# Attention scores of two heads from 64 rows of TensorE each, three split terms, two chunks in a burst

## The chip, the core and the metric

The kernel runs on one core of a Trainium2 chip. The metric is the device time of one execution in microseconds (us); three executions of the kernel before took 1080.8, 1082.9 and 1083.42 us, and their median, 1082.9 us, is the time before.

## What is computed

Sigmoid attention over 8 batches of 12 heads (448 tokens, 64 elements per head), followed by a feed-forward part without a nonlinearity:

```
scores = scale * np.matmul(q, k.transpose(0, 1, 3, 2)) - np.log(S)
attn = 1.0 / (1.0 + np.exp(-scores))
attn_out = np.matmul(attn, v)
x = attn_out.transpose(0, 2, 1, 3).reshape(B * S, H * D)
a = x @ w1
b = x @ w2
h = a * b @ w3
out = h @ w_out
```

The attention works in float32; the weights are float64 words, which the kernel decodes itself.

## The kernel before, in words

Two heads that stand side by side are a *pair*; there are 6 pairs per batch and 48 in all. The 448 tokens of k are cut into four *chunks*, three of 128 and one of 64 (the short chunk, number 3). For a chunk, TensorE makes the scores of both heads: a PSUM tile `sp` of two banks, one per head, with k's tokens down the partitions and 448 q tokens along. Two `sp` tiles exist, so that a third one waits until the first has been read. ScalarE takes the sigmoid, and TensorE multiplies the result with v (`attend`, accumulated in `av`).

The first 9 pairs are *plain*: q, k and the attention are float32, and one matmul per head makes a chunk's scores, from the 64 partitions in which that head's elements lie (line 196). The other 39 pairs are *split*: a value is the sum of a high part, rounded to fp32r, and the rest, its low part. Of q, a tile `qs` holds one head per column block, with the high part in partitions 0 to 63 and the low part in 64 to 127; k lies twice in `kh` (high) and twice in `kl` (low), once for either half of the partitions. So a matmul over all 128 rows multiplies one part of k with both parts of q, and a full chunk needs four matmuls (two heads, `kh` and `kl`, line 199). For this q and k are loaded twice each, by four DMAs per pair (line 135). The short chunk packs `kh` and `kl` into one tile `ks` of 128 columns (GpSimd, line 165), needs two matmuls (line 225), and has its two halves added by ScalarE and VectorE (`add_halves`, lines 186 and 187) before its sigmoids (`short_attention`). `attention` takes the sigmoid of a full chunk twice, rounded into `ah` and exact back into `sp`, and VectorE writes the difference to `al` (line 217).

Each pair has four *slots*, one per chunk, in the order 0, 3, 1, 2. In a slot TensorE's program has the scores of that slot's chunk; then 12 matmuls of the *filler* `up` (line 318), which is the first feed-forward product of the batch before; then the `attend` of the chunk of the slot before (line 255; four matmuls for a full chunk of a split pair, two for the short one). The orders of TensorE and of SP, which issues the DMAs, are written out by hand like this. From slot 34 on, a scheduler orders ScalarE, VectorE and GpSimd. `prepare` says in which slot a pair is loaded and split. Slot 36 is the first of the split pairs.

After the last pair TensorE finishes `up` (line 318), multiplies w3 with w_out (line 508) and makes the output (line 524).

Of the kernel before, what the change touches and what calls it, by code (L numbers as in the profile page):

```python
# [11 lines left out]
F32 = mybir.dt.float32  # L12
F32R = mybir.dt.float32r
U32 = mybir.dt.uint32
AF = mybir.ActivationFunctionType
ALU = mybir.AluOpType
# [9 lines left out]
def sigmoid_attention_bilinear_ffn(  # L26
# [16 lines left out]
    nc = tc.nc  # L43
    B, H, D, S = qT.shape
    DM, DF = w1.shape[0], w1.shape[1] // 2
    NT = B * S
    P = 128
    CHUNKS = [(c, min(P, S - c)) for c in range(0, S, P)]
    NC = len(CHUNKS)
    assert 2 * D == P and CHUNKS[-1][1] == D  # L50
    NPAIR = H // 2
# [4 lines left out]
    PLAIN = 9  # L56
# [3 lines left out]
    ps = ctx.enter_context(tc.tile_pool(name="ps", bufs=3, space=PSUM))  # L60
# [4 lines left out]
    def split(dst_hi, dst_lo, src, hi_engine, lo_engine):  # L65
        hi_engine(out=dst_hi, in_=src)  # L66
        lo_engine.tensor_tensor(out=dst_lo, in0=src, in1=dst_hi, op=ALU.subtract)  # L67
# [43 lines left out]
    pa = phase_a.enter_context(tc.tile_pool(name="pa", bufs=2, side="right"))  # L111
# [10 lines left out]

    def load_pair(b, hp):
        heads = slice(2 * hp, 2 * hp + 2)
        if b * NPAIR + hp < PLAIN:

            qk = pa.tile([P, 2, S], F32, name="qp", tag="qk", bufs=3)
            for i, src in enumerate((qT, kT)):
                nc.sync.dma_start(out=qk[:, i], in_=src[b, heads].rearrange("h d s -> (h d) s"))
            return qk[:, 0], qk[:, 1]  # L130
        qq = pa.tile([P, 2, S], F32, name="qq", tag="qk", bufs=3)
        kk = pa.tile([P, 2, S], F32, name="kk", tag="qk", bufs=3)
        for dst, src in ((qq, qT), (kk, kT)):
            for r in range(2):
                nc.sync.dma_start(
                    out=dst[r * D:(r + 1) * D], in_=src[b, heads].rearrange("h d s -> d h s")
                )
        return qq, kk

    def load_v(b, hp):  # L140
        vv = pa.tile([P, NC, 2 * D], F32, name="vv")
# [6 lines left out]
            nc.sync.dma_start(out=vv[r * D:(r + 1) * D, NC - 1], in_=v[b, full:, cols])  # L148
        return vv

    def split_pair(plain, qq, kk):

        if plain:
            return qq, kk, None, None
        qs = pf[0].tile([P, 2, S], F32R, name="qs")
        kh = pf[0].tile([P, 2, S], F32R, name="kh")
        kl = pf[0].tile([P, 2, S], F32R, name="kl")
        nc.vector.tensor_copy(out=qs, in_=qq)
        nc.vector.tensor_tensor(out=qs[D:], in0=qq[D:], in1=qs[D:], op=ALU.subtract)
        split(kh, kl, kk, nc.vector.tensor_copy, nc.gpsimd)  # L160

        ks = pf[0].tile([P, 2, P], F32R, name="ks")
        for j in range(2):
            for i, k in ((j, kh), (1 - j, kl)):
                nc.gpsimd.tensor_copy(out=ks[:, j, i * D:(i + 1) * D], in_=k[:, j, S - D:])
        return qs, kh, kl, ks

    def split_v(plain, vv):
        if plain:
            return vv  # L170

        vs = pf[0].tile([P, NC, 2, 2, D], F32R, name="vs")
        for j in range(2):
            split(vs[:, :, j, j, :], vs[:, :, j, 1 - j, :], vv[:, :, j * D:(j + 1) * D],
                  nc.vector.tensor_copy, nc.gpsimd)
        return vs

    def sigmoid(dst, src):
        n = src.shape[0]
        nc.scalar.activation(dst, src, AF.Sigmoid, bias=bias[:n], scale=scale)  # L180

    def add_halves(dst, src):

        for j in range(2):
            rows, others = slice(j * D, (j + 1) * D), slice((1 - j) * D, (2 - j) * D)
            nc.scalar.copy(out=dst[rows], in_=src[j][others])  # L186
            nc.vector.tensor_tensor(out=dst[rows], in0=src[j][rows], in1=dst[rows], op=ALU.add)  # L187

    def scores(qs, kh, kl, c):

        at, n = CHUNKS[c]
        sp = ps.tile([P, 2, 512], F32, name="sp", bufs=2)[:n, :, :S]
        for j in range(2):
            if kl is None:
                rows = slice(j * D, (j + 1) * D)
                nc.tensor.matmul(sp[:, j], kh[rows, at:at + n], qs[rows], start=True, stop=True)  # L196
                continue
            for m, k in enumerate((kh, kl)):
                nc.tensor.matmul(sp[:, j], k[:, j, at:at + n], qs[:, j], start=m == 0, stop=m == 1)  # L199
        return sp  # L200

    def attention(plain, sp):

        n = sp.shape[0]
        if plain:
            a = pa.tile([P, 2, S], F32, name="ap", tag="ah", bufs=3)[:n]
            sigmoid(a, sp)
            return (a,)
        ah = pa.tile([P, 2, S], F32R, name="ah", tag="ah", bufs=3)
        sigmoid(ah[:n], sp)  # L210
        sigmoid(sp, sp)
        if n < P:

            nc.vector.tensor_tensor(out=ah[n:], in0=sp, in1=ah[:n], op=ALU.subtract)
            return (ah,)
        al = pf[0].tile([P, 2, S], F32R, name="al")
        nc.vector.tensor_tensor(out=al, in0=sp, in1=ah, op=ALU.subtract)  # L217
        return ah, al

    def short_scores(ks, qs):  # L220


        sp = ps.tile([P, 2, 512], F32, name="sp", bufs=2)[:, :, :S]
        for j in range(2):
            nc.tensor.matmul(sp[:, j], ks[:, j], qs[:, j], start=True, stop=True)  # L225
        t = pf[0].tile([P, S], F32, name="st", bufs=1)
        add_halves(t, [sp[:, j] for j in range(2)])
        return t

    def short_attention(t):  # L230

        a = pa.tile([P, 2, S], F32R, name="ah", tag="ah", bufs=3)
        for j in range(2):
            rows = slice(j * D, (j + 1) * D)
            sigmoid(a[rows, j], t[rows])
        sigmoid(t, t)
        for j in range(2):
            rows, others = slice(j * D, (j + 1) * D), slice((1 - j) * D, (2 - j) * D)
            nc.vector.tensor_tensor(out=a[others, j], in0=t[rows], in1=a[rows, j], op=ALU.subtract)  # L239
        return (a,)  # L240

    def attend(c, ops, v, accs):

# [89 lines left out]
    def take(stream, n):  # L333
        for _ in range(n):
            next(stream, None)
# [30 lines left out]
    qks, vvs = {}, {}  # L366
    for p in range(2):
        qks[p] = load_pair(*pairs[p])
        load_job(p)
        if p == 0:  # L370
            vvs[0] = load_v(*pairs[0])
    splits, vs = {0: split_pair(0 < PLAIN, *qks.pop(0))}, {0: split_v(0 < PLAIN, vvs.pop(0))}
    xs = {b: [] for b in range(B)}
    filler = iter(())
    waiting = []
    accs = {}
    pf = []
# [14 lines left out]
    def prepare(p, i):  # L392

        n = p + 1
        change = n in (PLAIN, PLAIN + 1)
        if i == (2 if change else 1) and n < len(pairs):
            splits[n] = split_pair(n < PLAIN, *qks.pop(n))
        if i == 0 and change:
            qks[n] = load_pair(*pairs[n])
        if i == 1 and n < len(pairs):  # L400
            vvs[n] = load_v(*pairs[n])
        if i == NC - 1 and n < len(pairs):
            vs[n] = split_v(n < PLAIN, vvs.pop(n))
        n = p + 2
        if i == (0 if n < PLAIN else 2) and n not in (PLAIN, PLAIN + 1) and n < len(pairs):
            qks[n] = load_pair(*pairs[n])
# [3 lines left out]
    chunks = [0, NC - 1, *range(1, NC - 1)]  # L410
    ups = -(-(NF * 2 * NK * 3) // (NPAIR * NC))
    slot = 0
    for p, (b, hp) in enumerate(pairs):
        plain = p < PLAIN
        qs, kh, kl, ks = splits.pop(p)
        for i, c in enumerate(chunks):
            if slot == PLAIN * NC - 2:
                order.close()
                order.enter_context(tc.manual_schedule(engines={ET.PE, ET.SP}))
                phase_p.close()  # L420
                pf.append(phase_a.enter_context(tc.tile_pool(name="pf", bufs=2, side="right")))
            prepare(p, i)
            if not plain and i == 1:
                short = short_scores(ks, qs)
            else:
                sp = scores(qs, kh, kl, c)
                if not plain and i == 2:
                    waiting.append((slot + 1, p, NC - 1, short_attention(short)))
                waiting.append((slot + 1, p, c, attention(plain, sp)))
            for step, n in steps.get(slot, ()):  # L430
                step(n)
            if b > 0 and (hp, i) == (0, 2):
                take(filler, 10 ** 6)
                filler = up(b - 1, xs[b - 1], itertools.repeat("up"))
            take(filler, ups)
            if slot == 1:
                idle_products(6)
            attend_due(slot)
            slot += 1
# [21 lines left out]
    for jc in range(NF):  # L461
        take(filler, 10)
        for half in range(2):
            ms = slice(half * NM, (half + 1) * NM)
            src = w_out[jc * P:(jc + 1) * P].rearrange("p (m u) -> p m u", u=2)[:, ms]
# [33 lines left out]
    for ic in range(NF):  # L499
# [3 lines left out]
        for half in range(2):  # L503
            ms = slice(half * NM, (half + 1) * NM)
            acc = ps.tile([P, 512], F32, name="up", tag=next(banks), bufs=2)
            for jc in range(NF):
                for m, (a, w) in enumerate(((w3h, woh), (w3h, wol), (w3l, woh))):
                    nc.tensor.matmul(  # L508
                        acc[:, :NM], a[:, jc], w[:, jc, ms],
                        start=(jc == 0 and m == 0), stop=(jc == NF - 1 and m == 2),  # L510
# [52 lines left out]
```

## Time and profile before

| | |
|---|---|
| Span of the profiled execution, first to last instruction | 1079.5 us |
| Times of the runs | 1080.8, 1082.9, 1083.42 us |
| TensorE busy with matmuls | 1067.9 us |
| VectorE, ScalarE, GpSimd busy | 714.1, 563.4, 190.1 us |
| DMA packets' time, share of 16 engines' span | 40.6% |
| Mean granted clock of TensorE | 0.998 |

The span leaves out what lies ahead of the first and behind the last instruction, so a time is a little longer than a span. In the rows of the profile PE is TensorE's matmul, PEld its weight load, DVE VectorE, ACT ScalarE, POOL GpSimd, and L199 is line 199 of the kernel. "128\*128" is the part of the array that an instruction uses, rows by columns. The plain pairs reach to about 102 us of the span, the split pairs from there to about 715 us.

### The profile page before, as it was taken

To read this page: it belongs to the slowest core of one execution; us is meant where nothing else is said; L and a number is where in the kernel's file an instruction comes from. 1 tells how busy PE (TensorE), PEld (TensorE's weight loads), DVE (VectorE), ACT (ScalarE), POOL (GpSimd) and SP (SyncE) were. 2 spreads that over 40 slices of the span, in tenths; PEclk is the share of its full clock that TensorE was granted. 3 is DMA by queue.
4 is the path that set the end of the run, shared out by engine and by line. 5 is a ranking of instruction groups with operands and counts; after the bars stand their busy time and mean duration, and the time that the engine had idled before them with its cause. 6 is when DMAs were issued, how large, how long until landed. Compare 5 with 4: busy or idle time off the path is not lost.

```text
span 1079.5 us, 14155 instructions
## 1 busy us (share of the span) xinstructions
PE 1067.9 (99%) x5094; PEld 915.1 (85%) x5094; DVE 714.1 (66%) x1074; ACT 563.4 (52%) x789; POOL 190.1 (18%) x277
## 2 busy tenths in 40 slices
PE   8999899999999999999999999999999999999998
PEld 3256799999999999999999989999999888888886
DVE  5997978888878878888887877649862133223321
ACT  5855666776776677767767766653342011101100
POOL 0002432232233323232332224200000000000000
PEclk9999999999999999999999999999999999999999
DMA  8755434443543535344452543225471032233211
GB/s 257 231 166 146 103 95 122 124 132 104 140 118 103 141 107 135 112 131 115 116 154 79 135 122 92 68 75 180 137 243 39 20 127 93 84 127 127 88 49 49
DMA packets 100693, 129.15 MB, mean 120 GB/s; under 512 B 8016, under 2 KB 82960, under 8 KB 100624
## 3 DMA queue, kind: packets, MB, share of 16 engines
q1 hardware_dynamic: 100624, 128.25, 40.6%
q8 instruction: 40, 0.66, 0.3%
q14 instruction: 29, 0.24, 0.1%
HBM read 98.34 MB, written 29.88 MB: 119 GB/s over the span
## 4 chain that ended last, share of the span: by engine, by line
PE 94%; DVE 2%; DMA 1%; ACT 1%; issue 1%; SPq 0%; ACTq 0%
PE up L318 42%; PE up L524 21%; PE av L255 10%; PE sp L199 9%; PE up L508 6%; PE sp L196 2%; PE av L248 2%; PE sp L225 1%; DMA raw<-w 1%; DVE f L102 0%; ACT f L79 0%; DVE w L67 0%; DVE raw L99 0%; DVE f L94 0%; ACT ap L180 0%
## 5 line engine op out<-in xcount | busy, mean ns | idle before, releaser
L318 PE MATMUL up<-xh,w 128*128 128x448 f32 x1536 | 467.2, 368 | 0.0
L318 PEld LDWEIGHTS up<-xh,w 128*128 128x128 f32 x1536 | 288.8, 188 | 31.6 <-issue 5.9
L318 PE MATMUL up<-xl,w 128*128 128x448 f32 x768 | 281.2, 366 | 0.0
L524 PE MATMUL up<-w 128*128 128x512 f32 x1008 | 228.7, 389 | 0.0
L524 PEld LDWEIGHTS up<-w 128*128 128x128 f32 x1008 | 189.2, 188 | 39.2
L180 ACT ACTIVATE ah<-sp,bias 128x896 fp32r<-128x896 f32 x117 | 117.6, 1005 | 114.3 <-PE sp L199 113.5
L217 DVE TENSOR_TENSOR al<-sp,ah 128x896 fp32r<-128x896 f32 x117 | 127.5, 1090 | 50.0 <-ACT sp L180 49.0
L67 POOL TENSOR_TENSOR kl<-kk,kh 128x896 fp32r<-128x896 f32 x39 | 89.5, 2294 | 402.5 <-DVE kh L66 380.3
L318 PEld LDWEIGHTS up<-xl,w 128*128 128x128 f32 x768 | 144.4, 188 | 12.5
L534 DVE COPY o_sb<-up 128x512 f32<-128x512 f32 x42 | 29.0, 691 | 161.0 <-PE up L524 161.0
L66 ACT CAST w<-graw 128x1024 fp32r<-128x1024 f32 x28 | 29.4, 1056 | 175.9 <-PE up L524 170.5
L180 ACT ACTIVATE sp<-sp,bias 128x896 f32<-128x896 f32 x117 | 113.6, 971 | 0.0
L255 PE MATMUL av<-ah,vs 128*128 128x448 f32 x312 | 102.4, 368 | 3.8 <-DVE ah L239 2.7
L255 PE MATMUL av<-al,vs 128*128 128x448 f32 x234 | 86.1, 368 | 0.4 <-DVE al L217 0.4
L199 PE MATMUL sp<-qs,kh 128*128 128x448 f32 x234 | 86.3, 369 | 0.0
L67 POOL TENSOR_TENSOR vs<-vv,vs 128x256 fp32r<-128x256 f32 x78 | 68.2, 885 | 102.8 <-DVE vs L66 95.0
L199 PE MATMUL sp<-qs,kl 128*128 128x448 f32 x234 | 86.3, 369 | 0.0
L239 DVE TENSOR_TENSOR ah<-st,ah 64x448 fp32r<-64x448 f32 x78 | 59.3, 760 | 18.7 <-ACT st L180 16.8
L255 PEld LDWEIGHTS av<-ah,vs 128*128 128x128 f32 x312 | 58.5, 188 | 10.3 <-DVE ah L239 2.8
L79 ACT ACTIVATE f<-raw 128x768 f32<-128x768 f32 (+2 forms) x48 | 34.4, 716 | 48.3 <-DMA raw<-w_out 17.7
L186 ACT COPY t<-av 64x448 f32<-64x448 f32 x78 | 41.3, 529 | 32.3 <-PE av L255 31.2
L180 ACT ACTIVATE ah<-st,bias 64x448 fp32r<-64x448 f32 x78 | 52.2, 670 | 4.0 <-DVE st L187 2.0
(57 smaller groups left out, 1243.4 us busy)
## 6 DMA issues: line engine op xcount, KB each, us to landing
qq<-qT SPq DMA_DIRECT2D x78, 224.0 KB, 3.9
kk<-kT SPq DMA_DIRECT2D x78, 224.0 KB, 4.5
g_dram<-g SPq DMA_DIRECT2D x64, 224.0 KB, 2.0
graw<-g_dram SPq DMA_DIRECT2D x14, 1024.0 KB, 5.3
raw<-w SPq DMA_DIRECT2D x16, 768.0 KB, 5.3
out<-o_sb SPq DMA_DIRECT2D x42, 256.0 KB, 2.0
vv<-vL SPq DMA_DIRECT2D x48, 192.0 KB, 2.8
raw<-w3T SPq DMA_DIRECT2D x16, 512.0 KB, 4.1
```

What stands on the lines that cost most here:

```text
L66: hi_engine(out=dst_hi, in_=src)
L67: lo_engine.tensor_tensor(out=dst_lo, in0=src, in1=dst_hi, op=ALU.subtract)
L79: nc.scalar.activation(f, raw[..., 1].bitcast(F32), AF.Abs, scale=HW_SCALE)
L180: nc.scalar.activation(dst, src, AF.Sigmoid, bias=bias[:n], scale=scale)
L186: nc.scalar.copy(out=dst[rows], in_=src[j][others])
L199: nc.tensor.matmul(sp[:, j], k[:, j, at:at + n], qs[:, j], start=m == 0, stop=m == 1)
L217: nc.vector.tensor_tensor(out=al, in0=sp, in1=ah, op=ALU.subtract)
L239: nc.vector.tensor_tensor(out=a[others, j], in0=t[rows], in1=a[rows, j], op=ALU.subtract)
L255: nc.tensor.matmul(accs[j][:, :S], v[:, c, j].rearrange("p u d -> p (u d)"), a[:, j], start=first and m == 0, stop=last and m == len(ops) - 1,
L318: nc.tensor.matmul(acc[:, :S], w[:, fc, kc], x, start=(kc == 0 and m == 0), stop=(kc == NK - 1 and m == 2),)
L508: nc.tensor.matmul(acc[:, :NM], a[:, jc], w[:, jc, ms], start=(jc == 0 and m == 0), stop=(jc == NF - 1 and m == 2),)
L524: nc.tensor.matmul(acc[:, :TB], w[:, fc, ms], g[:, at, fc % NH], start=(fc == 0 and m == 0), stop=(fc == NF - 1 and m == 2),)
```

## The change

The split pairs make their scores in the way of the plain ones: each head from the 64 partitions where its elements lie. q and k are loaded once, into one tile `qk`, and split into `qkh` and `qkl` by one VectorE cast and one GpSimd subtraction. The scores of a chunk are three terms per head, high by high, low k by high q, high k by low q; the product of the two low parts is left out. The two heads alternate in the program. That makes six matmuls for any chunk, the short one too, and `ks`, `short_scores` and `short_attention` go; the short chunk takes the branch of `attention` that was there for it. The scores are now made in every second slot, for two chunks one behind the other: chunks 0 and 3 in the first slot of a pair, chunks 1 and 2 in the third. The diff, without what only goes (the old loads and `short_attention`):

```
@@ load_pair
+        qk = pa.tile([P, 2, S], F32, name="qk", bufs=3)
+        for i, src in enumerate((qT, kT)):
+            nc.sync.dma_start(out=qk[:, i], in_=src[b, heads].rearrange("h d s -> (h d) s"))
+        return qk
@@ split_pair
-        nc.vector.tensor_copy(out=qs, in_=qq)
-        nc.vector.tensor_tensor(out=qs[D:], in0=qq[D:], in1=qs[D:], op=ALU.subtract)
-        split(kh, kl, kk, nc.vector.tensor_copy, nc.gpsimd)
...
-                nc.gpsimd.tensor_copy(out=ks[:, j, i * D:(i + 1) * D], in_=k[:, j, S - D:])
+        split(high, low, qk, nc.vector.tensor_copy, nc.gpsimd)
+        return high, low
@@ scores
-            for m, k in enumerate((kh, kl)):
-                nc.tensor.matmul(sp[:, j], k[:, j, at:at + n], qs[:, j], start=m == 0, stop=m == 1)
+        terms = ((qk, qk),) if low is None else ((qk, qk), (low, qk), (qk, low))
+        for m, (k, q) in enumerate(terms):
+            for j in range(2):
+                rows = slice(j * D, (j + 1) * D)
+                nc.tensor.matmul(
+                    sp[:, j], k[rows, 1, at:at + n], q[rows, 0],
+                    start=m == 0, stop=m == len(terms) - 1,
+                )
@@ the loop over slots
-            if not plain and i == 1:
-                short = short_scores(ks, qs)
-            else:
-                sp = scores(qs, kh, kl, c)
-                if not plain and i == 2:
-                    waiting.append((slot + 1, p, NC - 1, short_attention(short)))
-                waiting.append((slot + 1, p, c, attention(plain, sp)))
+            for cc in (c,) if plain else chunks[i:i + 2] if i % 2 == 0 else ():
+                sps[cc] = scores(qk, low, cc)
+            waiting.append((slot + 1, p, c, attention(plain, sps.pop(c))))
```

The `attend` of the short chunk moves with it, from the fourth slot of its pair to the third.

Below, lines of the changed program have its own numbers: 179 is the scores (before 199 and 225), 216 `attend` (255), 279 the filler (318), 162 the sigmoid (180), 197 and 200 the low parts of the attention (239 and 217), 287 the copy of `up` (326), 290 the product `g` (329), 209 the plain `attend` (248). TensorE's program before, in the middle of the split pairs, where the first slot of a pair begins; the names are the tiles told of above:

```order
L255 MATMUL av<-al,vs 128x448
L255 MATMUL av<-ah,vs 128x448
L255 MATMUL av<-al,vs 128x448
L199 MATMUL sp<-qs,kh 128x448
L199 MATMUL sp<-qs,kl 128x448
L199 MATMUL sp<-qs,kh 128x448
L199 MATMUL sp<-qs,kl 128x448
L318 MATMUL up<-xh,w 128x448
```

The same place in the changed program, where "x2" is the two heads and the output's 64 or 128 rows are the chunk's tokens:

```order
L216 MATMUL av<-al,vs 128x448
L179 MATMUL sp<-qkh 128x448 x2
L179 MATMUL sp<-qkh,qkl 128x448 x2
L179 MATMUL sp<-qkl,qkh 128x448 x2
L179 MATMUL sp<-qkh 64x448 x2
L179 MATMUL sp<-qkh,qkl 64x448 x2
L179 MATMUL sp<-qkl,qkh 64x448 x2
L279 MATMUL up<-xh,w 128x448
```

Twelve matmuls over 64 rows stand where four over 128 stood; the second slot, which had two (line 225), and the fourth, which had four, have none, and the third has twelve as well.

The second place is ScalarE's program where the split pairs begin. Before (the row of line 79 is the magnitude of a weight block `raw` that was just loaded):

```order
L180 ACTIVATE ap<-sp,bias 128x896
L180 ACTIVATE ah<-sp,bias 128x896
L180 ACTIVATE sp<-sp,bias 128x2x448
L79 ACTIVATE f<-raw 128x768
L326 COPY a_sb<-up 128x448
L66 CAST xh<-av 128x448
L186 COPY st<-sp 64x448 x2
```

And in the changed program:

```order
L162 ACTIVATE ap<-sp,bias 128x896
L79 ACTIVATE f<-raw 128x768
L162 ACTIVATE ah<-sp,bias 128x896
L162 ACTIVATE sp<-sp,bias 128x2x448
L162 ACTIVATE ah<-sp,bias 64x896
L287 COPY a_sb<-up 128x448
L162 ACTIVATE sp<-sp,bias 64x2x448
L66 CAST xh<-av 128x448
```

The magnitude has moved ahead of the first split pair's sigmoids, and the short chunk's sigmoids follow those of chunk 0 at once, with no copies.

The third place is VectorE's program a little later. Before, ahead of the attend of the first pair's short chunk and of chunk 1:

```order
L158 CAST qs<-qq 128x896
L66 CAST kh<-kk 128x896
L159 TENSOR_TENSOR qs<-qq,qs 64x896
L67 TENSOR_TENSOR w<-f,w 128x768
L239 TENSOR_TENSOR ah<-st,ah 64x448 x2
L217 TENSOR_TENSOR al<-sp,ah 128x896
```

And in the changed program:

```order
L99 SCALAR_TENSOR_TENSOR raw<-raw 128x768
L200 TENSOR_TENSOR al<-sp,ah 128x896
L102 TENSOR_TENSOR f<-f,raw 128x768
L197 TENSOR_TENSOR ah<-sp,ah 64x896
L67 TENSOR_TENSOR w<-f,w 128x768
L67 TENSOR_TENSOR xl<-av,xh 128x448
L290 TENSOR_TENSOR g<-up,a_sb 128x448
```

The short chunk's low part now stands ahead of the weight split (line 67, `w<-f,w`), and before it stood behind it.

More of the change, by code (lines that the diff above doesn't have):

```diff
@@ L124, in load_pair @@
         heads = slice(2 * hp, 2 * hp + 2)
[L125 to L138, printed above, removed]
+        qk = pa.tile([P, 2, S], F32, name="qk", bufs=3)
+        for i, src in enumerate((qT, kT)):
+            nc.sync.dma_start(out=qk[:, i], in_=src[b, heads].rearrange("h d s -> (h d) s"))
+        return qk
     def load_v(b, hp):
@@ L149, in load_v, with split_pair @@
         return vv
-    def split_pair(plain, qq, kk):
+    def split_pair(plain, qk):
         if plain:
[L154 to L157, printed above, removed]
-        nc.vector.tensor_copy(out=qs, in_=qq)
-        nc.vector.tensor_tensor(out=qs[D:], in0=qq[D:], in1=qs[D:], op=ALU.subtract)
-        split(kh, kl, kk, nc.vector.tensor_copy, nc.gpsimd)
-        ks = pf[0].tile([P, 2, P], F32R, name="ks")
-        for j in range(2):
-            for i, k in ((j, kh), (1 - j, kl)):
-                nc.gpsimd.tensor_copy(out=ks[:, j, i * D:(i + 1) * D], in_=k[:, j, S - D:])
-        return qs, kh, kl, ks
+            return qk, None
+        high = pf[0].tile([P, 2, S], F32R, name="qkh")
+        low = pf[0].tile([P, 2, S], F32R, name="qkl")
+        split(high, low, qk, nc.vector.tensor_copy, nc.gpsimd)
+        return high, low
     def split_v(plain, vv):
@@ L187, in add_halves, with scores @@
             nc.vector.tensor_tensor(out=dst[rows], in0=src[j][rows], in1=dst[rows], op=ALU.add)
-    def scores(qs, kh, kl, c):
+    def scores(qk, low, c):
         at, n = CHUNKS[c]
         sp = ps.tile([P, 2, 512], F32, name="sp", bufs=2)[:n, :, :S]
-        for j in range(2):
-            if kl is None:
+        terms = ((qk, qk),) if low is None else ((qk, qk), (low, qk), (qk, low))
+        for m, (k, q) in enumerate(terms):
+            for j in range(2):
                 rows = slice(j * D, (j + 1) * D)
-                nc.tensor.matmul(sp[:, j], kh[rows, at:at + n], qs[rows], start=True, stop=True)
-                continue
-            for m, k in enumerate((kh, kl)):
-                nc.tensor.matmul(sp[:, j], k[:, j, at:at + n], qs[:, j], start=m == 0, stop=m == 1)
+                nc.tensor.matmul(
+                    sp[:, j], k[rows, 1, at:at + n], q[rows, 0],
+                    start=m == 0, stop=m == len(terms) - 1,
+                )
         return sp
@@ L218, in attention @@
         return ah, al
[L220 to L240, printed above, removed]
     def attend(c, ops, v, accs):
@@ L371, in sigmoid_attention_bilinear_ffn @@
             vvs[0] = load_v(*pairs[0])
-    splits, vs = {0: split_pair(0 < PLAIN, *qks.pop(0))}, {0: split_v(0 < PLAIN, vvs.pop(0))}
+    splits, vs = {0: split_pair(0 < PLAIN, qks.pop(0))}, {0: split_v(0 < PLAIN, vvs.pop(0))}
     xs = {b: [] for b in range(B)}
@@ L396, in prepare @@
         if i == (2 if change else 1) and n < len(pairs):
-            splits[n] = split_pair(n < PLAIN, *qks.pop(n))
+            splits[n] = split_pair(n < PLAIN, qks.pop(n))
         if i == 0 and change:
@@ L414, in sigmoid_attention_bilinear_ffn @@
         plain = p < PLAIN
-        qs, kh, kl, ks = splits.pop(p)
+        qk, low = splits.pop(p)
+        sps = {}
         for i, c in enumerate(chunks):
```

## The prediction

> **What bounds the kernel now.** I read the page first, then the stretch of the split pairs by windows, then the chain of waits in it, then the timeline of single matmuls.
>
> ```profile
> span 1079.5 us, 14155 instructions
> PE 1067.9 (99%) x5094; PEld 915.1 (85%) x5094; DVE 714.1 (66%) x1074; ACT 563.4 (52%) x789; POOL 190.1 (18%) x277
> PE 94%; DVE 2%; DMA 1%; ACT 1%; issue 1%; SPq 0%; ACTq 0%
> 125.00:627.00 502.00, 502.00 (x2457) 461.07 (x2456) 407.54 (x615) 357.89 (x508) 154.98 (x229) 1.00 0.45 121
> ```
>
> TensorE is busy for 99% of the span and makes 94% of the chain that ended last. The last row is the split pairs without their ends: in 502 us PE has not one idle moment (columns: us, then busy time of PE, PEld, DVE, ACT, POOL, the granted clock, DMA share), at full clock. So there a TensorE instruction more or less is paid or won in full, and work taken from VectorE, ScalarE, GpSimd or the DMA queues is worth nothing. The chain, at the same place of two successive pairs:
>
> ```profile
> 402.44 1.24 PE av L255 x6
> 404.50 2.44 PE up L318 x12
> ...
> 417.96 1.24 PE av L255 x6
> ```
>
> A pair takes 417.96 - 402.44 = 15.52 us. Its program has 76 matmuls: 48 of the filler, 14 of `attend`, 12 + 2 of the scores. 15.52 / 76 = **0.204 us** each; the twelve of the filler, 2.44 / 12 = 0.203, agree. There is no other time in a pair.
>
> **What goes and what comes.**
>
> ```profile
> L199 PE MATMUL sp<-qs,kh 128*128 128x448 f32 x234 | 86.3, 369 | 0.0
> L199 PE MATMUL sp<-qs,kl 128*128 128x448 f32 x234 | 86.3, 369 | 0.0
> L225 PE MATMUL sp<-qs,ks 128*128 128x448 f32 x78 | 22.5, 369 | 0.0
> ```
>
> 546 score matmuls go, 14 for each of 39 pairs: 14 x 0.204 = 2.86 us per pair. There come 4 chunks x 3 terms x 2 heads = 24 per pair, over 64 rows. No fp32r matmul over 64 rows is in the trace, but the plain pairs make their scores so in fp32 (two records per head there, each with its own weights):
>
> ```profile
> 60.85 0.37 PE L318 MATMUL up<-xh,w 128*128 128x448 f32 x1
> 61.14 0.13 PEld L248 LDWEIGHTS av<-ap,vv 64*64 64x64 f32 x1 [0.31 <-issue]
> 62.04 0.65 PE L196 MATMUL sp<-qp 64*128 64x448 f32 x2
> 62.15 0.19 PEld L196 LDWEIGHTS sp<-qp 64*128 64x128 f32 x2
> 62.52 0.54 PE L196 MATMUL sp<-qp 64*128 64x448 f32 x2
> 62.99 0.19 PEld L318 LDWEIGHTS up<-xh,w 128*128 128x128 f32 x1 [0.65 <-issue]
> 62.99 0.47 PE L318 MATMUL up<-xh,w 128*128 128x448 f32 x1
> 63.10 0.19 PEld L318 LDWEIGHTS up<-xl,w 128*128 128x128 f32 x1
> 63.31 0.37 PE L318 MATMUL up<-xl,w 128*128 128x448 f32 x1
> ```
>
> Two things stand here. First, the two heads run side by side: both matmuls start in one merged row at 62.04, both weight loads at 62.15, both next matmuls at 62.52. A record streams for 62.52 - 62.15 = 0.37 us, once for both heads. So 24 matmuls are 12 steps. What a step takes in fp32r no row shows. From below, half of the fp32 record, 0.187; from above, 0.221, if each head adds the 0.017 by which a full matmul now exceeds 0.187 (0.204 - 0.187). I take **0.204**, that of the fp32r matmul over the whole array, the nearest row: 12 x 0.204 = 2.45 us. Alone, this wins 2.86 - 2.45 = 0.41 us per pair, 15.9 us in all.
>
> Second, **a change of the array's shape costs time**. After the filler's matmul of 60.85 the next would come at 61.05; the first of another shape comes at 61.14, 0.09 later. After the scores' last record (62.52 + 0.37 = 62.89) the filler comes at 62.99, 0.10 later. And the first weights then lie open: the filler's matmul issued at 62.99 has its weights at 63.10, when the load for its successor begins, so this load of 0.19 us shows 0.11, and the next matmul starts 63.31 - 62.99 = 0.32 later, not 0.204. A change to 128 columns thus costs 0.09 + 0.11 = **0.20 us**. The chain says the same of a whole plain slot:
>
> ```profile
> 63.07 2.66 PE up L318 x12
> 67.58 2.66 PE up L318 x12
> ```
>
> 4.51 us, less 12 x 0.204 for the filler and 4 x 0.37 for two steps each of scores and `attend`, leaves 0.58 for three changes, one of them to 64 columns. Is it the shape, or the step between fp32r and fp32? At the start of the program two chunks of scores follow one another, fp32 both, the second the short one:
>
> ```profile
> 6.98 0.54 PE L196 MATMUL sp<-qp 64*128 64x448 f32 x2
> 7.45 0.14 PEld L196 LDWEIGHTS sp<-qp 64*64 64x64 f32 x2 [0.65 <-issue]
> ```
>
> 6.98 + 0.37 = 7.35, and the 64\*64 begins at 7.45: the same 0.10, so it is the shape, and 64\*128 to 64\*64 counts as one. With half the columns I put the open load at half, 0.05, and this change at 0.15.
>
> The split pairs have one shape, 128\*128, and so no change. Now each burst is entered and left, 2 x 2 x 0.20, and the first burst has the short chunk behind chunk 0, 0.15: **0.95 us per pair**. That is more than the 0.41 won: 15.52 - 0.41 + 0.95 = 16.06 us, +0.54, times 39 is **+21 us**. The burst of two chunks halves the changes, but they would have to cost under 0.41 / 5 = 0.08 each to pay.
>
> The Trainium skill, page "TensorEngine Tiling (Array Packing)", section "Key Properties", says that changing the tiling mode, though not changing the tile within a mode, drains the TensorE; it gives no price. Without that rule the sum would be -16 us; with it and the rows above, +21. The trace agrees.
>
> **Edits that cost nothing here.** Per pair, two loads of q and k, VectorE's low part of `qs`, GpSimd's copies into `ks` and the short chunk's halves go. TensorE's full rows cover all of it, before as after. Of waits there are two kinds to look at.
>
> (a) A burst needs both `sp` tiles.
>
> ```profile
> L180 ACT ACTIVATE ah<-sp,bias 128x896 fp32r<-128x896 f32 x117 | 117.6, 1005 | 114.3 <-PE sp L199 113.5
> L180 ACT ACTIVATE sp<-sp,bias 128x896 f32<-128x896 f32 x117 | 113.6, 971 | 0.0
> L217 DVE TENSOR_TENSOR al<-sp,ah 128x896 fp32r<-128x896 f32 x117 | 127.5, 1090 | 50.0 <-ACT sp L180 49.0
> ```
>
> Chunk 0's scores end 0.20 + 3 x 0.204 = 0.8 us into the pair. Two sigmoids each for chunks 0 and 3 stand together on ScalarE, 4 x 0.99 = 3.95 (the short chunk has as many elements per partition), then 1.09 on VectorE: 5.9 us plus latencies. The second burst begins after 1.77 (first burst) + 24 x 0.204 (filler) + 8 x 0.204 (`attend`), at 8.3. Between stand at most the weight decodes, which come once in two pairs. Slack about 2 us: I cost it at nothing.
>
> (b) The beginning of the split pairs, where PE does wait now:
>
> ```profile
> 106.82 0.89 ACT L79 ACTIVATE f<-raw 128x768 f32<-128x768 f32 x1 [1.21 <-DMA raw<-w]
> 116.44 2.74 DVE L67 TENSOR_TENSOR w<-f,w 128x768 fp32r<-128x768 f32 x1
> 117.08 0.37 PE L318 MATMUL up<-xh,w 128*128 128x448 f32 x1
> 119.89 0.47 PE L255 MATMUL av<-ah,vs 128*128 128x448 f32 x1 [2.43 <-DVE ah L239]
> 122.30 0.57 PE L255 MATMUL av<-al,vs 128*128 128x448 f32 x1
> 122.88 1.49 PE sp L199 x4
> 124.37 2.98 PE up L318 x12
> ```
>
> From 117.08 to 122.30 six matmuls take 5.2 us in place of 1.2, behind the weight split of 2.74 us; and the clock falls, so that the 16 behind take 4.47 in place of 3.27. Together 5.2 us. In the new order VectorE has the short chunk's part ahead of that split. But ScalarE's magnitude, which waited for its load until 106.82, now stands ahead of chunk 0's sigmoids: they end at 107.7 + 2.0 = 109.7, the decode of about 4 us stands ahead of `al`, which ends near 113, and PE is there at about 110. So some 3 us are lost in another place. I take **-2 us**; -5 if all is gone, +3 if both waits come.
>
> Sum: 1079.5 + 21 - 2 = 1098.5 us of span. The median of the runs lies 1082.9 - 1079.5 = 3.4 above the span, so **1102 us**.
>
> **Rivals.**
> - *Shape changes are free between fp32r matmuls*, and the drain belongs to fp32. Then -16 - 2: 1065 us. For it: no row shows such a change. Against: 60.85 to 61.14 drains an fp32r matmul. 6%. It is the one that ends on the other side, and decides where a change costs under 0.08.
> - *The heads run one after the other in fp32r*: 12 x 0.204 x 39 = +95 us, 1197. Against: rows 62.04 and 62.52. 5%.
> - *A head's next weights are not loaded while its own matmul streams*, so that each step shows 0.11 of a load: 12 x 0.11 x 39 = +51, 1153. Against: the loads of 62.15 run under the matmuls of 62.04 on the same rows. 4%. The Trainium skill states such a rule on its page "TensorE: Matmul & The Clock Gate", Part 3, "The mechanism": a weight load overlaps a running matmul only where the row groups differ. The trace disagrees, at 62.15 and at 63.10 alike.
> - *Bursts wait for `sp`*, where decodes or copies eat the 2 us of slack: at 0.25 us for each of 78 bursts +20, 1122. 12%.
>
> **How the numbers follow.** The forecast has 73%. Inside it the step's bounds are 12 x 39 x 0.017 = 8 us to either side, and the beginning gives 3 us less to 5 more: 1091 to 1115. The range reaches up over the waiting bursts, **1089 to 1125**; the first three rivals and part of the fourth lie outside. About 0.3%, 1079.7 to 1086.1, is what a measurement tells from no change. Faster: 0.07, the first rival and a little; same: 0.04; slower: 0.89.
>
> **What would show it.** In the profile after, a pair of 16.1 us; the first matmul of a burst about 0.3 us behind its forerunner and the first of the filler behind a burst the same, with 0.32 to the next; two heads' matmuls within 0.01 us of each other, steps of 0.19 to 0.22; no idle row that names `sp`'s readers. A pair under 15.5 us would make the price of a change wrong; steps of 0.3 or 0.4, the side by side.

## The result, and the profile after

| | before | after |
|---|---|---|
| Median of the runs | 1081.97 us (4 runs, 1080.8 to 1083.42) | 1097.76 us (4 runs, 1096.95 to 1098.93) |
| Span of the profiled execution, and its time | 1079.5 us | 1097.1 us, 1098.93 us |

The changed kernel is slower: the ratio of the times is 1.0153, with a 95% interval of 1.0136 to 1.017. The forecast was 1102 us, so sign and size came out as predicted. Two of its terms were wrong, though, and cancelled one another. One execution of a kernel told of below (four bursts, 1341.42 us) and one of the kernel before (6025.22 us) stand far outside the others and are left out.

The head of the page of the changed kernel, and the engines' shares of the chain that ended last:

```profile
span 1097.1 us, 14262 instructions
PE 1083.4 (99%) x5484; PEld 882.0 (80%) x5484; DVE 604.8 (55%) x879; ACT 514.5 (47%) x672; POOL 154.2 (14%) x121
PE 95%; DVE 1%; DMA 1%; issue 1%; ACT 1%; SPq 0%; ACTq 0%
```

VectorE lost 109 us of work, ScalarE 49 and GpSimd 36, and the span grew by 17.6. None of the three set the time; TensorE did, before and after. The two kernels' busy time by stretch says where the time came from. The rows give the stretch, its length, the busy time (and instructions) of PE, PEld, DVE, ACT and POOL, the granted clock, the DMA share and GB/s. Before:

```profile
100.00:125.00 25.00, 21.91 (x96) 17.32 (x95) 21.11 (x28) 13.74 (x19) 11.38 (x15) 0.94 0.51 131
125.00:700.00 575.00, 573.94 (x2806) 526.51 (x2805) 464.58 (x699) 410.45 (x583) 176.28 (x259) 1.00 0.43 117
```

After:

```profile
100.00:125.00 25.00, 18.57 (x83) 13.11 (x82) 16.16 (x21) 11.57 (x14) 5.66 (x5) 0.80 0.30 98
125.00:700.00 575.00, 575.00 (x3108) 484.18 (x3107) 354.54 (x505) 355.05 (x460) 141.31 (x109) 1.00 0.28 87
```

From 125 us on, TensorE is busy without a gap at full clock, and the same pairs still take longer. In the 25 us where the split pairs begin it idles longer than before, and its mean clock is 0.80: it was granted at 0.50 from 114.2 to 124.2 us. These are the two places.

**The pairs.** The chain of waits in the middle of the split pairs (start, length, engine, tile, line, count) is TensorE alone. Before:

```profile
395.91 0.83 PE sp L199 x4
396.74 2.44 PE up L318 x12
...
411.43 0.83 PE sp L199 x4
```

After:

```profile
400.09 1.41 PE sp L179 x9
401.50 2.67 PE up L279 x12
...
405.00 2.44 PE up L279 x12
...
408.29 1.42 PE sp L179 x12
409.71 2.63 PE up L279 x12
...
416.01 1.41 PE sp L179 x12
```

A pair takes 411.43 - 395.91 = 15.52 us before and 416.01 - 400.09 = 15.92 after. The sigmoid's readers and everything else stand beside it. Twelve matmuls over full rows take 2.44 us wherever they follow others of their shape, and 2.63 to 2.67 behind a burst: about 0.20 for leaving it. A burst is six steps, 6 x 0.204 = 1.22, and takes 1.41: about 0.20 for entering it. Two bursts, four changes of shape, about 0.80 us. TensorE's timeline of the first burst shows each of them ("x2" is the two heads):

```profile
399.72 0.37 PE L216 MATMUL av<-al,vs 128*128 128x448 f32 x1
400.02 0.47 PE L179 MATMUL sp<-qkh 64*128 64x448 f32 x2
400.33 0.36 PE L179 MATMUL sp<-qkh,qkl 64*128 64x448 f32 x2
400.53 0.37 PE L179 MATMUL sp<-qkl,qkh 64*128 64x448 f32 x2
400.73 0.37 PE L179 MATMUL sp<-qkh 64*64 64x448 f32 x2
...
401.13 0.37 PE L179 MATMUL sp<-qkl,qkh 64*64 64x448 f32 x2
401.43 0.47 PE L279 MATMUL up<-xh,w 128*128 128x448 f32 x1
401.75 0.36 PE L279 MATMUL up<-xl,w 128*128 128x448 f32 x1
```

Steps of 0.20 for two heads at once; 0.30 into the burst and 0.31 to its second step, 0.30 out of it and 0.32 to the filler's second matmul, which is 0.10 more than a step in all four places. And between 64\*128 and 64\*64, at 400.53 and 400.73, nothing: the forecast had 0.15 there.

The median of all pairs' periods is 15.91 us after and 15.53 before: 0.38 x 39 = 14.8 us.

**The beginning.** The first split pair takes 25.9 us from its first score to the next pair's, 10.0 over a common one. Before, the first two took 20.1 and 16.8, together 5.9 over. That is 4.1 us worse. One wait of 1.6 us, which the kernel before had near 628 us, is gone. 14.8 + 4.1 - 1.6 = 17.3, of 17.6 us. The rest is the difference of two more: in this execution the split pairs begin 1.0 us later than before (103.58 and 102.56 us), a lag that is there by 22 us of the span, behind a stretch at a granted clock of 0.50 from 15.2 to 18.4 us; and what follows the last pair's beginning is shorter again. So the 4.1 us, and the 1.0, are those of one execution, at a mean clock of 0.994; the other three had 0.997.

### The profile page after: what moved, and what is told of

Same layout as the page of the kernel before. It is cut to its first block, busy times and chain, and to the rows that moved or that the text cites. A ratio compares the mean times of both kernels' runs of the same rounds, so it can differ in the third digit from the quotient of the medians.

```text
span 1097.1 us, 14262 instructions
## 1 busy us (share of the span) xinstructions
PE 1083.4 (99%) x5484; PEld 882.0 (80%) x5484; DVE 604.8 (55%) x879; ACT 514.5 (47%) x672; POOL 154.2 (14%) x121
## 4 chain that ended last, share of the span: by engine, by line
PE 95%; DVE 1%; DMA 1%; issue 1%; ACT 1%; SPq 0%; ACTq 0%
PE up L279 43%; PE up L482 21%; PE sp L179 12%; PE av L216 10%; PE up L466 6%; PE av L209 2%; DMA raw<-w 1%; ACT ap L162 0%; DVE vs L66 0%; DVE f L102 0%; ACT w L66 0%; DVE raw L99 0%; SPq L127 0%; ACT f L79 0%; DVE raw L86 0%
## 5 line engine op out<-in xcount | busy, mean ns | idle before, releaser
L279 PE MATMUL up<-xh,w 128*128 128x448 f32 x1536 | 475.7, 373 | 0.0
L162 ACT ACTIVATE ah<-sp,bias 128x896 fp32r<-128x896 f32 (+1 forms) x156 | 157.0, 1007 | 175.5 <-PE sp L179 175.5
L162 ACT ACTIVATE sp<-sp,bias 128x896 f32<-128x896 f32 (+1 forms) x156 | 152.3, 976 | 0.0
L67 POOL TENSOR_TENSOR qkl<-qk,qkh 128x896 fp32r<-128x896 f32 x39 | 83.8, 2149 | 204.7 <-DVE qkh L66 109.5
L216 PE MATMUL av<-ah,vs 128*128 128x448 f32 x312 | 108.9, 369 | 2.9 <-DVE xl L67 2.9
L179 PE MATMUL sp<-qkh 64*128 64x448 f32 (+1 forms) x312 | 65.7, 418 | 0.0
L179 PE MATMUL sp<-qkl,qkh 64*128 64x448 f32 (+1 forms) x312 | 57.8, 366 | 0.0
L179 PE MATMUL sp<-qkh,qkl 64*128 64x448 f32 (+1 forms) x312 | 57.2, 363 | 0.0
L197 DVE TENSOR_TENSOR ah<-sp,ah 64x896 fp32r<-64x896 f32 x39 | 42.3, 1084 | 20.4 <-ACT sp L162 19.9
L169 DVE TENSOR_TENSOR t<-av,t 64x448 f32<-64x448 f32 x78 | 48.5, 622 | 5.4 <-ACT t L168 3.0
```

The costliest lines, as they stand in the source:

```text
L179: nc.tensor.matmul(sp[:, j], k[rows, 1, at:at + n], q[rows, 0], start=m == 0, stop=m == len(terms) - 1,)
L216: nc.tensor.matmul(accs[j][:, :S], v[:, c, j].rearrange("p u d -> p (u d)"), a[:, j], start=first and m == 0, stop=last and m == len(ops) - 1,
L279: nc.tensor.matmul(acc[:, :S], w[:, fc, kc], x, start=(kc == 0 and m == 0), stop=(kc == NK - 1 and m == 2),)
```

## The experiments: what a change of shape costs

My theory: 0.20 us for each change between 128 and 64 rows, four per pair, the heads side by side, and no wait for `sp`. The rivals: the loss belongs to something else in the burst (its waits, the order of the heads), or to the step between fp32 and fp32r.

### The scores over all 128 rows

No change of shape: each chunk has three matmuls over 128 rows and 128 columns. They multiply the same tiles, but both heads' elements are summed in one product, so the scores are others; all that follows is done with them.

```
-        for m, (k, q) in enumerate(terms):
-            for j in range(2):
-                rows = slice(j * D, (j + 1) * D)
-                nc.tensor.matmul(sp[:, j], k[rows, 1, at:at + n], q[rows, 0], ...)
...
+        at = min(at, S - P)
+        nc.tensor.matmul(sp[:, 0], qk[:, 1, at:at + P], qk[:, 0], start=True, stop=False)
+        nc.tensor.matmul(sp[:, 1], low[:, 1, at:at + P], qk[:, 0], start=True, stop=True)
+        nc.tensor.matmul(sp[:, 0], qk[:, 1, at:at + P], low[:, 0], start=False, stop=True)
```

> The changed kernel, with its 24 score matmuls per split pair over 64 rows replaced by 12 over all 128 rows and 128 columns, so that the array's shape never changes in the split pairs; the heads' elements are mixed in these products (high by high and high by low of both heads into one bank, low by high into the other), so the scores are not the reference's. Bursts of two chunks, the waits on sp and everything else stay. Theory, the changes of shape cost 0.20 us each and nothing else is lost: a pair is 74 matmuls of 0.204 us = 15.1 us in place of 15.92, times 39 is -32 us: 1066 us, and 16 below the kernel before. Rival, the loss is in the burst (two sp tiles awaited, two chunks' sigmoids in a row): a pair stays at 15.9 us and the time at 1098 us.

Measured: 1078.84 us (10 runs, 1076.7 to 1079.62; ratio to before 0.998, 0.9971 to 0.999). The chain of waits of its profiled execution, the first score of three successive bursts and one filler:

```profile
410.93 0.21 PE sp L177
...
412.17 2.44 PE up L281 x12
418.27 0.21 PE sp L177
426.04 0.21 PE sp L177
```

A pair without a wait takes 426.04 - 410.93 = 15.11 us and its filler 2.44 behind the burst too. Against 15.91 that is 0.80 for four changes, 0.20 each: the theory's number. The time, however, missed what was expected by 12 us. Its pairs' mean is 15.49, not 15.11; some two in five take 15.6 to 17.3. In the timeline, TensorE's row of a matmul that waited in one of these:

```profile
200.45 0.47 PE L218 MATMUL av<-al,vs 128*128 128x448 f32 x1 [0.44 <-DVE al L202]
```

VectorE's `al` is late: in the chain of waits it ran from 199.30, behind a weight decode and the casts of the next pair. A little later in the same pair the second chunk of the burst starts at 202.07 in place of 201.78, until VectorE has made the next `al` and with it read the `sp` tile; five bursts between 130 and 700 us lose 0.3 us in this way. At 15.9 us per pair there is room for this, at 15.1 there is not: the slack that the forecast gave the bursts (about 2 us) was enough for the changed kernel, and is not for pairs that are 0.8 us shorter. So dropping the changes of shape brought 19 us, not the 31 that 0.80 in 39 pairs comes to.

### Four bursts per pair

```
-            for cc in (c,) if plain else chunks[i:i + 2] if i % 2 == 0 else ():
+            for cc in (c,):
```

> The changed kernel with the scores of each chunk made in the slot of that chunk, so four bursts per split pair with six matmuls each, eight changes of shape in place of four. Theory of the shape: 4 more changes of 0.20 us, 39 pairs: +31 us, 1129 us, a pair of 16.7 us. Rival, the loss comes from waiting for two sp tiles at once: single chunks wait less, and the time falls towards 1082 us.

Measured: 1122.01 us (three of four runs, 1121.81 to 1123.14; ratio 1.0385, 1.0364 to 1.0407). Three of four successive bursts in its chain of waits, with the filler behind each, and the burst that stands a pair behind the first (the short chunk's is at 412.65):

```profile
400.29 0.81 PE sp L179 x6
401.10 2.63 PE up L279 x12
...
404.14 0.80 PE sp L179 x4
404.94 2.64 PE up L279 x12
...
412.65 0.75 PE sp L179 x4
413.40 2.63 PE up L279 x12
...
416.85 0.82 PE sp L179 x6
```

The fillers show the 0.20 behind every burst. The median pair is 16.60, 0.69 more than with two bursts, for four more changes: 0.17 each. The short chunk's burst takes 0.75 where the others take 0.81, which fits a load of 64 columns left open in place of 128 and takes some 0.06 of the missing 0.11. The price follows the number of changes, as the theory has it.

### One head after the other

```
-        for m, (k, q) in enumerate(terms):
-            for j in range(2):
+        for j in range(2):
+            for m, (k, q) in enumerate(terms):
```

> The changed kernel with the three terms of one head written ahead of the three of the other, in place of alternating heads. If TensorE starts its matmuls in the order of the program and one waits only for the one before it on its own rows, then of the 12 matmuls of a burst three pairs of neighbours run side by side, 9 steps in place of 6: 3 x 0.204 x 78 = +48 us, 1146 us. Rival, TensorE finds the other head's matmul further down in its queue: 6 steps still, 1098 us. If heads never ran side by side in the changed kernel, no change either.

Measured, one run: 1100.05 us, span 1098.3, a pair 15.93. The rival was right. In the program three matmuls of head 0 stand ahead of three of head 1, and the timeline still shows pairs of them:

```profile
398.98 0.47 PE L179 MATMUL sp<-qkh 64*128 64x448 f32 x2
399.29 0.37 PE L179 MATMUL sp<-qkh,qkl 64*128 64x448 f32 x2
399.49 0.37 PE L179 MATMUL sp<-qkl,qkh 64*128 64x448 f32 x2
```

In every burst from 130 us on the first matmuls of the two heads start 0.010 us apart, where the changed kernel has 0.003 to 0.004. So the two programs do differ on the chip, and the six steps stay. I read this as TensorE taking the other head's matmul from further down its queue, over the idle half of the rows; the trace shows starts, not the queue. Alternating the heads by hand, as the change does, is not what lets them run side by side.

### Single shapes, one behind the other

Behind the last filler, this kernel runs rows of matmuls of one shape after another, on tiles that are there; the output is not touched. The calls it adds, several to a line:

```
+    full(qk, 4); full(qk, 3, D); full(qk, 4); one_head(qk, 3); full(qk, 4); heads(qk, 3)
+    full(qk, 4); heads(qk, 2); heads(qk, 2, D); full(qk, 4); full(f32, 3); full(qk, 4)
+    heads(f32, 3); full(qk, 4); heads(qk, 2); heads(f32, 2); heads(qk, 2); full(qk, 4)
```

`full` uses 128 rows, `one_head` the 64 rows of one head, `heads` those of both; `D` means 64 columns in place of 128, `f32` the tile before it is split.

> The changed kernel with 65 more matmuls (98 records) behind the last split pair, on tiles that are there, into a bank that nobody reads; between groups stand four fp32r matmuls over 128 rows and 128 columns. Start to start, a plain step of fp32r is 0.204 us. Theory, only a change between 64 and 128 rows drains the array: 128 to 64 columns over 128 rows 0.204 into the group; 64 rows by one head 0.30 into the group and 0.204 inside, by two heads the same; 64 x 128 to 64 x 64 0.204; fp32 over all rows 0.20 into the group; two fp32 products one behind the other in one shape 0.37 apart. Rival A, a change of columns drains too: 0.30 at the 64 columns over 128 rows. Rival B, a change between fp32r and fp32, or the end of every fp32 product, drains: 0.30 into the fp32 group over all rows, and 0.47 between fp32 products of one shape, which would explain the 0.10 that the plain chunks of one shape class showed before. Time some 17 us above 1098.

Measured, one run: 1114.52 us. Two successive rows of the timeline, where one head's 64 rows follow 128:

```profile
739.51 0.37 PE L407 MATMUL sp<-qkh 128*128 128x448 f32 x1
739.81 0.47 PE L407 MATMUL sp<-qkh 64*128 64x448 f32 x1
```

In the trace's records of TensorE's matmuls (their starts, in us, one digit finer): over 128 rows, the last of 128 columns at 738.100 and the first of 64 at 738.303, which is a plain step of 0.203. To one head's 64 rows 739.51 to 739.81, 0.30, and 0.307 to the next, then 0.207; out of them 0.293 and 0.306. With both heads the same numbers, in steps of 0.20. From 64\*128 to 64\*64 in fp32r 743.754 to 743.958, 0.204. From fp32r to fp32 over 128 rows 745.180 to 745.384, 0.204. So in fp32r it is **the number of rows that costs**, twice 0.10 on each crossing; neither the columns nor the step to fp32 does. This places the forecast's error: 64\*128 to 64\*64 was priced by a row in fp32. What "shape" means here is the rows and columns that the profile gives for an instruction; how the array was set up inside is not in it.

### The same in fp32, and the heads written one after the other

Again the calls, several to a line:

```
+    full(qk, 4); heads(f32, 2); heads(f32, 2, D); heads(f32, 2); full(qk, 4)
+    full(f32, 2); full(f32, 2, D); full(f32, 2); full(qk, 4)
+    for j, cols in ((0, P), (1, D)):
+        for _ in range(3):
+            product(qk, j, D, cols)
```

> The changed kernel with other matmuls behind the last split pair, into a bank that nobody reads. Two heads in fp32, two products of 128 columns, two of 64, two of 128; the same over all 128 rows; then in fp32r three products of one head with 128 columns written ahead of three of the other head with 64 columns. Theory, in fp32 a change of columns within 64 rows drains as it did between the first two plain chunks (0.10), though in fp32r it does not: 0.47 start to start into the group of 64 columns in place of 0.375. Rival, the 0.10 there came from something else than the columns: 0.375. For the last group: if TensorE takes the other head's matmul from further down its queue, a row of 64 x 64 starts beside the first of 64 x 128, three steps in all, 0.6 us; if it keeps to the written order, 64 x 64 starts only beside the third, five steps, 1.0 us. Time some 15 us above 1098.

Measured, one run: 1112.18 us. In fp32 a change of columns does cost:

```profile
740.31 0.54 PE L407 MATMUL sp<-qk 64*128 64x448 f32 x2
740.78 0.59 PE L407 MATMUL sp<-qk 64*64 64x448 f32 x2
```

Within 64 rows 740.308 to 740.781, 0.473, where the steps before it are 0.375, and 0.426 to the next: 0.10 and 0.05 more, just what the forecast put down. Over 128 rows 746.17 to 746.64, 0.47. So the row of the forecast (6.98 to 7.45) was read rightly, and does not carry over from fp32 to fp32r. The last loop writes three matmuls of 64\*128 on one head's rows and then three of 64\*64 on the other's. They start at 750.788 (64\*128), 750.798 (64\*64), 751.058, 751.102, 751.265 and 751.313: again side by side, even with two widths, and against the written order. The group is through in three steps, as the first of the two theories for it has it.

## The experiments: the beginning, and whether more is to be had

### The last weight blocks earlier, in the changed kernel

The plan had eight of the sixteen blocks of the first half of the weights decoded between slot 25 and slot 34; here one starts in each slot from 24 on, so that the plain pairs carry them.

```
-    starts = [1 + 3 * i for i in range(8)] + [first + 1 + 4 * i // 3 for i in range(8)]
+    starts = [1 + 3 * i for i in range(8)] + [first + i for i in range(8)]
-        steps.setdefault(s + (3 if s < first else 2), []).append((split_job, i))
+        steps.setdefault(s + (3 if s < first else 1), []).append((split_job, i))
```

> The changed kernel with the last eight weight blocks decoded one per slot from slot 24 (before: at 25, 26, 27, 29, 30, 31, 33, 34) and each split one slot later, so that no weight is loaded, decoded or split where the split pairs begin, and all their loads lie in the early buffers. Theory, the 10 us that the first split pair loses (25.9 us in place of 15.9) are the wait for the last block's load and its decode ahead of the first al: the first pair takes 16 to 18 us and the time falls by 8 to 10, to 1088 to 1090 us. Rival, the first split pair's own preparation (the split of q, k and v on VectorE and GpSimd) is what is late: 1098 us still. Second rival, VectorE has no room for one decode per slot, and the plain pairs wait instead: 1094 us or more.

Measured: 1093.46 us (ratio to before 1.0108, 1.0092 to 1.0124), 4.3 under the changed kernel: between the theory and the second rival. The first split pair takes 16.2 us, as expected, but starts at 107.5 in place of 103.6, for two new waits stand among the plain pairs. The timeline's row of the first:

```profile
74.52 0.47 PE L279 MATMUL up<-xh,w 128*128 128x448 f32 x1 [2.65 <-ACT a_sb L287]
```

ScalarE's copy of `up` stands behind a cast of weights, which waits for VectorE's decode.

### The same in the kernel before

> The kernel before with the same eight blocks earlier. Theory as for the changed kernel: its first two split pairs take 20.1 and 16.8 us in place of 15.5 each, 5.9 us lost, and those go: 1076 us, faster than both kernels. Rival, the plain pairs wait for VectorE instead: 1082 us.

Measured: 1081.46 us (11 runs; ratio 0.9997, 0.9988 to 1.0006): no difference. The first pairs now take 15.95 and 15.53, and the plain ones pay for it:

```profile
74.81 0.74 PE L318 MATMUL up<-xh,w 128*128 128x448 f32 x1 [2.64 <-ACT a_sb L326]
```

In the 40 us from 60 to 100, VectorE works 37.67 us before and 38.87 us here: there is hardly room to move the decodes into. The rival was right. With this plan the changed kernel stays 12.0 us behind the kernel before, so its worse beginning does not decide the comparison.

### A second buffer for a block's load

The changed kernel again, with the plan as it was.

```
-            raw = pd.tile([P, NK, P, 2], U32, name="raw", bufs=1)[:, :src.shape[1]]
+            raw = pd.tile([P, NK, P, 2], U32, name="raw", bufs=2)[:, :src.shape[1]]
```

> The changed kernel with two buffers in place of one for the late weight loads, so that the last block's load need not wait until VectorE has decoded the one ahead of it. Theory, that load (5.2 us, from 101.89 to 107.06) stands in the chain of the first split pair: its magnitude starts some 5 us earlier, and the first pair loses 4 to 5 us less: 1093 us. Rival, VectorE's queue is the bound there and the load only ran beside it: 1098 us.

Measured, one run: 1091.15 us, span 1089.4. From 100 to 125 us TensorE's clock is 1.00 and the waits are short:

```profile
100.00:125.00 25.00, 21.92 (x116) 15.92 (x115) 14.67 (x22) 13.54 (x17) 9.45 (x5) 1.00 0.21 66
111.57 0.47 PE L216 MATMUL av<-al,vs 128*128 128x448 f32 x1 [0.95 <-DVE al L200]
113.43 0.44 PE L216 MATMUL av<-ah,vs 128*128 128x448 f32 x1 [1.39 <-DVE xl L67]
```

So the last block's load, which must wait until VectorE is through with the buffer's last content, starts the loss. The first split pair takes 20.0 us in place of 25.9: 5.9 us come back with the one buffer, and the same two waits are left, shorter, with one of 0.74 us for `sp` at 103.37. The span is 7.7 us shorter, but 1.8 of it is there at 21 us already, before the late loads, and is not the buffer's. In the kernel before, which loses 5.9 us in its first two pairs, a second buffer was not tried.

### The weights' low parts on GpSimd, in the kernel before

A way to free VectorE: GpSimd makes the weights' low parts. First with the plan as it was, then with the decodes about a slot earlier.

```
-        split(wh[n][:, at, cs], wl[n][:, at, cs], fs.pop(i), nc.scalar.copy, nc.vector)
+        split(wh[n][:, at, cs], wl[n][:, at, cs], fs.pop(i), nc.scalar.copy, nc.gpsimd)
```

> The kernel before with only those 16 subtractions moved to GpSimd, the weight blocks at their old slots. Theory, the last block's load still stands in the chain (5.6 us), but the weight split of 2.74 us ahead of the short chunk's low part is gone: 2 to 4 us won, 1078 to 1080 us. Rival, as above, VectorE slows as much as it is relieved: 1082 us.

Measured: 1093.54 us (ratio 1.0114, 1.0098 to 1.0129). In the groups of instructions, one step of the decode on VectorE, before and then here:

```profile
L94 DVE SCALAR_TENSOR_TENSOR f<-f,raw 128x768 uint32<-128x768 uint32 x16 | 15.3, 959 | 0.4
```

```profile
L94 DVE SCALAR_TENSOR_TENSOR f<-f,raw 128x768 uint32<-128x768 uint32 x16 | 24.8, 1551 | 0.4
L67 POOL TENSOR_TENSOR w<-f,w 128x768 fp32r<-128x768 f32 x16 | 32.4, 2024 | 75.6 <-ACT w L66 75.6
```

VectorE gives away a subtraction of 1.09 us per block, 17.4 us in all, and its five other steps of the decode that grow take 19.1 us more. What counts is who starts first: of the 16 steps of line 94, the six that start behind one of GpSimd's subtractions (0.02 to 0.56 us) take 2.45 to 2.64 us and end 0.8 us behind it; the other ten, two of which GpSimd joins later, take 0.95 to 0.98. Neither theory nor rival had a loss of this size. With the earlier plan:

```
-    starts = [1 + 3 * i for i in range(8)] + [first + 1 + 4 * i // 3 for i in range(8)]
+    starts = [1 + 3 * i for i in range(8)] + [first + 1 + i for i in range(7)] + [first + 9]
```

> The kernel before with the low parts of w1 and w2 (16 subtractions of 128x768) made by GpSimd in place of VectorE, and the last eight weight blocks decoded at slots 25 to 31 and 33 in place of 25 to 34 with gaps. Theory, where the split pairs begin VectorE's queue and the last block's late load are the bound, and the plain pairs have no room on VectorE for more: with 16 x 0.95 us off VectorE both go, and the 5.9 us of the first two split pairs are won: 1076 us, faster than both kernels. Rival, GpSimd's subtractions slow VectorE where they run together, as the weight split of 2.74 us beside GpSimd shows, and nothing is won: 1082 us or more.

Measured: 1089.6 us (ratio 1.0076, 1.0063 to 1.0088); the longest of its waits, 4.87 us at 102.26, is TensorE's for VectorE's `g`. Here the rival was right. No version with the whole computation was found that beats both kernels.

## Why the prediction was right, and where it was not

- **Two heads side by side, 0.204 a step: right.** The timeline's steps are 0.20, and 14 + 24 matmuls of scores changed as counted: the win of 0.41 per pair stands, since 15.11 (scores over full rows, also 12 steps) is 0.41 under 15.52.
- **A change between 128 and 64 rows costs 0.20: right**, and shown by removal (0.80 for four) and by doubling (0.69 for four more). The two parts of it, about 0.10 of drain and 0.10 of a load that lies open, show at every crossing. The rival that called changes free between fp32r matmuls was wrong for the rows. It held for the columns.
- **"64\*128 to 64\*64 counts as one": wrong.** The step priced this change at 0.15 us, 5.9 us in 39 pairs, from a row in fp32. In fp32r it costs nothing (400.53 to 400.73; the two kernels with single shapes say the same). The pair's term was +0.54 and measured +0.38, so +21 became +14.8.
- **The beginning, -2 with bounds of -5 and +3: wrong**, by measure +4.1. The mechanism was seen in its first half: the magnitude ahead of chunk 0's sigmoids, waiting for its load, and `al` behind the decode. The load came when expected (107.08 for the magnitude), but `al` was done at 115.0 and not 113, and a second wait came behind it, which the step didn't have, nor a fall of the clock. The timeline of the four engines in the changed kernel:

```profile
107.08 0.91 ACT L79 ACTIVATE f<-raw 128x768 f32<-128x768 f32 x1 [3.44 <-DMA raw<-w]
110.66 2.33 POOL L67 TENSOR_TENSOR qkl<-qk,qkh 128x896 fp32r<-128x896 f32 x1 [9.61 <-DVE qkh L66]
110.96 2.18 DVE L66 CAST vs<-vv 128x256 fp32r<-128x256 f32 x1
113.93 1.08 DVE L200 TENSOR_TENSOR al<-sp,ah 128x896 fp32r<-128x896 f32 x1
115.06 0.74 PE L216 MATMUL av<-al,vs 128*128 128x448 f32 x1 [3.57 <-DVE al L200]
117.89 0.62 DVE L67 TENSOR_TENSOR xl<-av,xh 128x448 fp32r<-128x448 f32 x1
118.66 0.71 PE L216 MATMUL av<-ah,vs 128*128 128x448 f32 x1 [2.85 <-DVE xl L67]
118.96 0.28 DVE L66 CAST vs<-vv 128x256 fp32r<-128x256 f32 x1
```

  The cast of `vs` took 2.18 us behind GpSimd's subtraction, which had begun 0.31 us earlier, and 0.28 at 118.96. VectorE has no pause between 108.0 and 115.0, so these 1.9 us are what made `al` late. And the second head's matmul needs the second `av` buffer, which the last plain pair still holds until VectorE has read it into `xl`. `xl` now stands behind the weight split. In the kernel before it came early:

```profile
108.69 0.62 DVE L67 TENSOR_TENSOR xl<-av,xh 128x448 fp32r<-128x448 f32 x1
```

  The forecast's own quoted order shows `xl` there, and I looked only at who makes an input for the next matmul, not at who frees its output. During the first wait the clock falls to 0.50, until 124.2 us, and the steps behind the second wait take 0.37 in place of 0.20. From start to start the waits cost 3.7 and 3.4 us and the slow steps 2.6, together 9.7 of the 10.0 us; the step had some 3 us, for the first wait alone. That the load starts it is shown by the second buffer, with which the clock stays at 1.00; what the cast and `xl` each cost is read from the timeline and was not tried apart.
- **Waits for `sp`: none, right.** No matmul of the scores (line 179) has a wait in the split pairs' timeline. The slack is small, as the scores over full rows show: with pairs of 15.1 us VectorE's `al` is late, and some bursts wait.
- **The weights of a head load while its own matmul streams: right**, by the steps of 0.20.

By the forecast's own terms: span 1079.5 + 21 - 2 = 1098.5, measured 1097.1. The 6 us too many in the pairs and the 6 too few at the beginning cancelled. That the sum came so close is luck; the sign is not, since the price of the rows alone, about 0.80 against 0.41 won per pair, gives it. The forecast then added 3.4 us from span to time, where this kernel's executions have 1.8.

## What to carry to other kernels

Packing two 64-row products side by side pays only if the run of them is long: crossing between 128 and 64 rows cost 0.20 us here, one whole matmul of 448 columns, so a burst must save more than two of those, and these saved one. Price such a crossing from a row in the same data type, and in the stretch where the work changes order ask of each matmul both what makes its inputs and who still reads the buffer it writes. A kernel bound by TensorE does not gain from 194 us less work on the other engines.

## What I had not expected of the hardware

- TensorE did not keep to the written order of two heads on separate rows: 750.788 and 750.798 start side by side though three matmuls apart in the program as it is written. The Trainium skill, page "TensorE: Matmul & The Clock Gate", Part 3, "The mechanism", has matmuls strictly in order; the trace disagrees for matmuls on different row groups.
- A change of columns drains in fp32 (0.47 in place of 0.375) and not in fp32r (0.203). The Trainium skill, page "TensorEngine Tiling (Array Packing)", "Key Properties", says that a change of mode drains; in fp32r the trace agrees for the rows and not for the columns, in fp32 it agrees for the columns. Rows from fp32 to fp32 were not tried.
- A VectorE instruction that starts behind one of GpSimd can wait until that one is done, and one that starts ahead of it does not: 2.45 to 2.64 us against 0.95 to 0.98 for the step of line 94, and 0.81 to 2.23 us for the three casts of `vs` in the changed kernel that start behind a GpSimd subtraction, against 0.28 to 0.29 for the 37 that GpSimd joins later. The Trainium skill, page "GPSIMD Engine Reference", "1. Specifications", states that the two share their SBUF interfaces, with contention for VectorE instructions in a 2-port mode or with two SBUF inputs; the trace agrees for line 94, which has two inputs, and shows the price. Whether the cast, with one input, ran in such a mode it does not show.
